# Attention and routed experts on one core: the first expert slot begins four query tiles later

## The chip, the cores and the metric

One core of one Trainium2 chip runs the whole kernel. The metric is the device time of one execution in microseconds (us); lower is better.

## The reference, cut to what is computed

```python
# attention: B=8 batches, H=8 heads, S=576 positions, D=64
scores = q @ k.T / sqrt(64)
scores = where(scores >= scores.max(-1) - 0.02, scores, -1e9)   # tau = 0.02
attn = softmax(scores); x = (attn @ v) -> [N=4608, DM=512]      # 8 heads side by side
# mixture of experts, one expert for each token: E=8, F=1024
logits = x @ w_gate + modality_bias[modality_id]                # [N, 8]
e = argmax(logits); g = softmax(logits)[e]
out[n] = g[n] * (relu(x[n] @ w1[e]) @ w2[e])
```

## The kernel before, in words

**Attention.** The work goes by head pairs, 32 of them (p = 0 to 31, four to a batch), and each pair by nine query tiles, so there are 288 tiles (or steps) n = 9p + i. For each tile TensorE computes the scores into one of two PSUM tiles (`qk_half`, L391), VectorE takes their maximum (`softmax_a`, L419, L421), ScalarE the exponential (L424), VectorE the product with the mask (`softmax_b`, L437). TensorE then transposes the result (`tr`, L465; ScalarE copies it, L475), and later multiplies it with v (`pv_half`, L499). Tiles 2 to 97 run two at a time: L391 and L465 of both, then one block of other matmuls, until the next two.

**Preparing a pair.** q and k of the next pair are loaded (`load_qk`, L116, L118), transposed on TensorE (L314 for the remainder, L329 for the main part), copied out by ScalarE (L316, L317, L332), and split on GpSimd into a high and a low half (`split_pool`, L302 and L303: tiles `nk`, `nq`, `qb`). Four DMAs on SyncE's queue put the halves of k (`km<-nk`, L338) and four those of q (`q<-nq`, L341) where the L391 matmuls of the next pair read them. Pair 7 begins with tile 63.

**From attention to experts.** Finished rows of x go to DRAM (`xs`, L558, L571). When a batch is done, its tokens are routed: the gate (L583 on), the counts, and five indirect DMAs of GpSimd that scatter each token's row number and weight into a table ordered by expert (`tab`, L651). `pick` chooses the expert with the most tokens left.

**Slots.** A slot gives one expert up to 256, 320 or 512 tokens of a batch while attention goes on: seven slots, the first two with 256 (batch 1) and 320 (batch 2) tokens, the rest with 512; what is left follows after attention. `slot()` builds a slot's work: `expert` (L763) reads the expert's number into a register; `rows` (L767, L769) loads the rows of the table (`tb<-tab`); `gather(t)` (L781) fetches 128 tokens of x with an indirect DMA of GpSimd (`xg<-xs,tb`); `xt(t)` (L795) transposes them; `wload` (L805 for w1, L809 for w2) loads a weight block into one of 4 `raw` buffers; `wsplit` (L825, L827) splits it on GpSimd into high and low halves, tiles `w1h`, `w1l` with 3 buffers each and `w2h`, `w2l` with 5; `l1` (L841) and `l2` (L868) are the matmuls. For the first slot these are 48 *pieces*: 32 of l1 (8 blocks f0 to f7, four pieces each, three matmuls of 256 columns a piece) and 16 of l2 (three matmuls of 512 columns). L852 and L853 turn a finished block of l1 into `hh` and `hl`.

**What sets the order.** Each engine runs its instructions in the order in which the program writes them, and nothing reorders them; so an instruction that waits holds back all that stands behind it on its engine, the DMAs that it issues included. What goes where in that order is set by a table `C` of numbers (L45 to L47): `at(t, f)` places work at step t, `put(n, f)` into the block after tile n. `begins` (L991) is the step at which each slot's pieces start: 64 for the first, 100 for the second. `draw` spreads a slot's pieces evenly over the steps from its begin to the next one's. Choosing, expert, rows, gathers and transposes stand at fixed distances ahead of the begin (L1026, L900 to L904), the weight blocks at those of the list `wS` or `wL` (L1052), each load `wl` = 3.5 steps ahead of its split.

Of the kernel before, what the change touches and what calls it, by code (L numbers as in the profile page):

```python
# [29 lines left out]
def tile_attn_moe(  # L30
# [13 lines left out]

    C = {'prep': [0, 1, 2], 'tr0': 6, 'pv0': 7, 'tr1': 12, 'sums': 13, 'pv1': 13, 'x': 14, 'gate': [15, 16, 17, 18], 'route': 18, 'routeb': 21, 'E0': 28, 'lag': 3, 'first': ((1, 0), (1, 1), (1, 2), (1, 3), (2, 0)), 'lld': {(1, 5): 15, (1, 6): 15.6, (1, 7): 16.2, (2, 5): 16.8, (2, 6): 17.4, (2, 7): 18}, 'late': ((1, 5), (1, 6), (1, 7), (2, 5), (2, 6), (2, 7)), 'pick': -14, 'vld': 6, 'qkld': -5, 'pre': 2.5, 'wl': 3.5, 'rows': -11, 'gat': [-9.5, -8.5, -7, -5], 'xt': [-6, -5, -4, -2], 'lc': 21, 't3': 84, 'neg': 1.0, 'draw': [2, 2, 2, 2, 1, 2, 2, 1, 2], 'last': 36, 'part': 84, 'join': 11, 'drawj': [2, 2, 2, 2, 2, 2, 0, 2, 2], 'gatej': [15, 15, 17, 18], 'te': 8, 'f0': 19, 'sc': 1, 'warm': 24,  # L45
         'wS': [-6, -4.7, -3.4, 3, 12.5, 14, 15.5, 21.5, 4.2, 5.4, 6.6, 7.5, 22.7, 23.8, 24.9, 25.8],
         'wL': [-5.5, -4, -2.5, 2.7, 12, 13.3, 14.6, 21, 3.8, 4.9, 6, 7.1, 15.8, 22.2, 23.4, 24.6], 'ask': 4, 'exp': -12.5, 'two': 98, 'end': (12, 13, (15, 16), (13.5, 13.6, 14.1, 14.2), 14.5, 15, 16.5), 'xf': 9, 'early': [], 'parts': ((((7, 0, 2), (9, 2, 5)), ((11, 0, 2), (13, 2, 5))), (((6, 0, 2), (8, 2, 4), (10, 4, 5)), ((12, 0, 2), (14, 2, 5)))), 'xp': ((15, 16), (16, 17)), 'prepp': ((0, 1, 2), (0, 0, 2)), 'trp': ((7, 11), (6, 12))}  # L47
    nc = tc.nc
    B, H, S, D = q.shape
    NE = wg.shape[1]  # L50
# [12 lines left out]
    W = 512  # L63
# [7 lines left out]
    SIDE = [(WH, 1), (WM, 2)] + [(W, b) for b in range(3, B)]  # L71
# [16 lines left out]
    xp = ctx.enter_context(tc.tile_pool(name="xp", bufs=1))  # L88
# [570 lines left out]
    def pick(w):  # L659

        a = tiny.tile([1, NE], F32, name="pk_a", bufs=1)
        nc.vector.scalar_tensor_tensor(out=a, in0=done, scalar=float(-U), in1=base[0][0:1, :],
                                       op0=ALU.mult, op1=ALU.add)
        nc.vector.scalar_tensor_tensor(out=a, in0=a, scalar=float(w), in1=iota_1, op0=ALU.is_ge, op1=ALU.mult)
        r = tiny.tile([1, 1], F32, name="pk_r", bufs=1)
        nc.vector.tensor_reduce(out=r, in_=a, axis=AX.X, op=ALU.max)
        nc.vector.tensor_scalar(out=a, in0=iota_1, scalar1=r, scalar2=None, op0=ALU.is_equal)
        t2 = tiny.tile([1, NE], F32, name="pk_d", bufs=1)
        nc.vector.scalar_tensor_tensor(out=t2, in0=a, scalar=float(U), in1=done, op0=ALU.mult, op1=ALU.mult)
        si = tiny.tile([1, 2], I32, name="pk_i")  # L670
        nc.vector.tensor_reduce(out=si[:, 1:2], in_=t2, axis=AX.X, op=ALU.max)
        nc.vector.tensor_scalar(out=si[:, 0:1], in0=r, scalar1=-1.0, scalar2=0.0, op0=ALU.add, op1=ALU.max)
        nc.vector.scalar_tensor_tensor(out=done, in0=a, scalar=float(w // U), in1=done, op0=ALU.mult, op1=ALU.add)
        return si[:, 0:1], si[:, 1:2]
# [73 lines left out]
    def slot(where, group, nrow, WT=W, wq=lambda: wp, nbuf=(4, 3, 5), lo_eng=None, xq=None, late=(), lined=False, pack=False):  # L748


        ev, pe, xts = [], [], []
        box = {}
        F2 = FC // 2
        TT = -(-WT // P)
# [21 lines left out]
        def gather(t):  # L776
            def f():
                xg = xt_pool().tile([P, DM], F32, name="xg", bufs=nx[1])
                box[("xg", t)] = xg

                nc.gpsimd.indirect_dma_start(  # L781
                    out=xg, out_offset=None, in_=xs[0:nrow, :],
                    in_offset=bass.IndirectOffsetOnAxis(ap=box["tb"][:, t, 0:1].bitcast(U32), axis=0),
                    bounds_check=nrow - 1, oob_is_err=False)
            return f

        def xt(t):
            def f():
                if t == 0:
                    room()  # L790
                ps = tbank()
                xg = box.pop(("xg", t))
                w = TP(t)
                for c in range(KC):
                    nc.tensor.transpose(out=ps[:, c * w:(c + 1) * w], in_=xg[0:w, c * P:(c + 1) * P],  # L795
                                        identity=ident[0:w, 0:w])
                ts = slice(t * P, t * P + w)
                split(ps[:, 0:KC * w].rearrange("a (c p) -> a c p", c=KC), box["xh"][:, :, ts], box["xl"][:, :, ts])
            return f
# [100 lines left out]
        else:  # L900
            ev += [(None, expert, C['exp']), (None, rows, C['rows'])]
        for t in range(TT):
            ev.append((t - 8, gather(t)) if xq else (None, gather(t), C['gat'][t - TT]))
            xts.append((C['xt'][t - TT] if not xq else t, xt(t)))  # L904
        for f_ in range(FC):
            t0 = (ta if f_ < F2 else tc_ - F2 * u1) + f_ * u1
# [16 lines left out]
        if xq:  # L923
            ev = [(e[0] - e[2], e[1]) if len(e) > 2 and e[0] > -8 else e for e in ev]
# [10 lines left out]
    PB = NPAIR * NI  # L935
# [5 lines left out]
    def at(t, f):  # L941
        events.setdefault(t, []).append(f)

    def put(n, *fs):
        extra.setdefault(n, []).extend(fs)

    for p in range(NPR):
        n0 = p * NI
# [39 lines left out]
            put(n0 + rb, lambda b=p // NPAIR: route_b(b))  # L988


    begins = [b * PB + C['E0'] + C['lag'] * max(0, z - 2) for z, (_, b) in enumerate(SIDE)]  # L991
    draw = [0] * (NSTEP + 2)
    for z, (w, _) in enumerate(SIDE):
        n0 = begins[z]
# [13 lines left out]
    def step_of(k):  # L1008

        if k >= upto[-1]:  # L1010
            return NSTEP + 2 + (k - upto[-1]) / 2
        n = bisect.bisect_right(upto, k) - 1
        return n + (k - upto[n]) / max(1, draw[n])
# [7 lines left out]
    for n0, (w, nb) in zip(begins, SIDE):  # L1021
        cells = {}

        def choose(cells=cells, w=w):
            cells["c"] = pick(w)
        at(n0 + C['pick'], choose)  # L1026
        late = C['late'] if n0 == begins[-1] else ()
        ev, pe, xts = slot(lambda cells=cells: cells["c"], lambda: group_bank(), nb * S, w, late=late)
        at(min(n0 - 0.45, NSTEP + 1), lambda pe=pe: work_q.extend(f for _, f in pe))
        for x, f in xts:  # L1030
            put(n0 + x, f)
        times = [t for t, _ in pe]
        k0 = sum(FC * KC + FC * -(-x // P) for x, _ in SIDE[:begins.index(n0)])

        def when(u):

            if u < 0:
                return n0 + u * C['neg'] * W / w
            k = bisect.bisect_right(times, u) - 1
            nxt = times[k + 1] if k + 1 < len(times) else times[k] + 0.5  # L1040
            x = k + min(1, (u - times[k]) / (nxt - times[k]))
            kf = math.floor(x)
            a, b = step_of(k0 + kf), step_of(k0 + kf + 1)
            return a + (x - kf) * (b - a) - 0.5
        for e in ev:

            if e[0] is None:
                t = n0 + e[2]
            elif n0 in begins[:-1]:

                which, f_ = e[3]
                t = n0 + C['w' + 'SL'[w == W]][8 * which + f_ - 8] - e[2]  # L1052
            elif e[2] and e[3] in C['lld']:
                t = NSTEP + C['lld'][e[3]]
            else:
                t = when(e[0]) - e[2] - (1.5 if e[3] in late and e[3][0] == 1 else 0)
            at(t, e[1])

    def last_slot(j, z):

        def where():
            si = fin["si"]
            return si[0:1, z, j:j + 1], si[0:1, z, MAXC + j:MAXC + j + 1]
        return slot(where, lambda: group_bank(), N, SIZES[z], lambda: fin["wp"], (8, 4, FC),
                    lambda which, f_: nc.vector if which == 1 else nc.gpsimd, (lambda: fin["xp"], (2, 4)),
                    lined=z + j == 0, pack=2 * SIZES[z] == W)
# [3 lines left out]
    def group_bank():  # L1070
        if "pm" in fin:
            return fin["pm"].tile([P, 512], F32, name="pm", tag="pm")
        return tbank(True)
# [18 lines left out]
    for z in range(3):  # L1092
        for j in range(ALWAYS[z]):
            for e in sum(last_slot(j, z), []):
                t = t0 + e[0] if len(e) == 2 else min(t0 + e[0], F0 + e[2])
                if z + j == 0 and getattr(e[1], "key", 0) in C['first']:
                    t = F0 - 8.15 + C['first'].index(e[1].key) / 1000
# [12 lines left out]
    with tc.manual_schedule(engines={ET.PE, ET.Pool}):  # L1110
# [5 lines left out]
        for n in range(NSTEP + LAG):  # L1116
# [8 lines left out]
            two = 2 <= n < C['two']  # L1125
# [82 lines left out]
```

## Time and profile before

| | us |
|---|---|
| median of 3 runs | 1025.12 (1023.4 to 1026.83) |
| the profiled execution: its own time | 1026.37 |
| the profiled execution: first to last instruction (span) | 1024.6 |
| PE (TensorE) busy in the span | 990.1 |
| VectorE, ScalarE, GpSimd busy | 687.6, 628.4, 534.2 |

The profile is of one execution. PE stands for the matmuls, PEld for TensorE's weight loads, DVE for VectorE, ACT for ScalarE, POOL for GpSimd, SPq for SyncE's issuing of DMAs; L391 is line 391 of the kernel. A row's time is counted from the span's start.

### The profile page before, as it was taken

The numbers are of one execution on the slowest core, as the hardware profiler recorded it, in microseconds if no ns is written. First come the engines' busy times: TensorE is split into PE (matmuls) and PEld (weight loads), VectorE is DVE, ScalarE is ACT, GpSimd is POOL, SyncE is SP. The second block draws the span as 40 slices with busy tenths as digits, with TensorE's granted clock in tenths as the row PEclk, the third lists the DMA queues.
The fourth block names the chain that finished last, engine by engine and source line by source line (L and its number), as shares of the span: only waits on it lengthen the run. The fifth ranks groups of instructions, "written<-read, shape, count | busy, mean of one in ns | idle before, by whom it ended". The sixth has DMA issues, their size and how long they took to land.

```text
span 1024.6 us, 20353 instructions
## 1 busy us (share of the span) xinstructions
PE 990.1 (97%) x6556; PEld 795.6 (78%) x6556; DVE 687.6 (67%) x1697; ACT 628.4 (61%) x1407; POOL 534.2 (52%) x781
## 2 busy tenths in 40 slices
PE   7999989999999999999999999999999999999996
PEld 6777768778877887888778887788778868888885
DVE  6888968787767776777687777777676765333422
ACT  6777767666666666666667666666666635334430
POOL 3363466386637554645555554646566363624311
PEclk9999999999999999999999999999999999999998
DMA  6677586668657766586646566767666236634301
GB/s 153 141 164 168 121 188 170 173 151 205 174 131 161 202 158 151 105 218 155 171 115 158 138 165 148 143 155 205 159 118 173 79 111 171 221 104 146 108 15 43
DMA packets 207315, 152.10 MB, mean 148 GB/s; under 512 B 100510, under 2 KB 168094, under 8 KB 207200
## 3 DMA queue, kind: packets, MB, share of 16 engines
q1 hardware_dynamic: 200000, 131.53, 53.1%
q0 software_dynamic: 7200, 19.18, 6.0%
q8 instruction: 54, 0.88, 0.4%
q14 instruction: 61, 0.50, 0.2%
HBM read 80.06 MB, written 19.48 MB: 97 GB/s over the span
## 4 chain that ended last, share of the span: by engine, by line
PE 78%; DVE 9%; issue 8%; ACT 3%; POOL 1%; DMA 0%; another core or an unknown queue 0%; POOLq 0%; ACTq 0%; DVEq 0%
PE bk L499 16%; PE s L391 15%; PE bk L841 11%; PE bk L465 10%; PE bk L868 9%; PE pm L868 5%; PE pm L841 5%; DVE nm L419 3%; DVE pr L437 3%; PE bk L329 2%; ACT e L424 2%; PE bk L490 1%; PE bk L795 1%; PE bk L551 1%; PE bk L583 1%
## 5 line engine op out<-in xcount | busy, mean ns | idle before, releaser
L419 DVE TENSOR_REDUCE nm<-s 128x1 f32<-128x576 f32 x288 | 216.3, 753 | 113.3 <-PE s L391 106.7
L437 DVE SCALAR_TENSOR_TENSOR pr<-s,nm,e 128x576 f32<-128x576 f32 x288 | 231.7, 815 | 65.2 <-ACT e L424 56.8
L424 ACT ACTIVATE e<-s,nm 128x576 f32<-128x576 f32 x288 | 214.3, 744 | 67.1 <-DVE nm L419 55.8
L391 PE MATMUL s<-km,q 128*128 128x288 f32 x1024 | 197.0, 314 | 11.1 <-DVE pr L437 7.2
L475 ACT COPY ptm<-bk 128x512 f32<-128x512 f32 x256 | 149.3, 583 | 54.9 <-PE bk L465 50.2
L465 PE MATMUL bk<-ident,pr 128*128 128x128 f32 x1152 | 174.0, 273 | 0.5 <-DVE hl L853 0.3
L391 PEld LDWEIGHTS s<-km,q 128*128 128x128 f32 x1024 | 147.1, 189 | 27.8 <-DVE pr L437 16.6
L465 PEld LDWEIGHTS bk<-ident,pr 128*128 128x128 f32 x1152 | 140.0, 140 | 30.0 <-issue 7.2
L499 PE MATMUL bk<-ptm,v_m 128*64 128x320 f32 (+1 forms) x1024 | 141.1, 412 | 2.5 <-DVE hl L853 2.5
L827 POOL TENSOR_TENSOR w2l<-raw,w2h 128x512 fp32r<-128x512 f32 x77 | 98.3, 1285 | 31.8 <-ACT w2h L823 27.7
L499 PEld LDWEIGHTS bk<-ptm,v_m 128*64 128x64 f32 x1024 | 68.5, 137 | 53.1 <-issue 8.1
L883 POOL DMA_INDIRECT out_dram<-y,tb x37 | 38.0, 1026 | 123.4 <-DVE y L881 89.7
L454 ACT COPY rp<-pr 128x64 f32<-128x64 f32 x271 | 59.9, 248 | 43.6 <-DVE pr L437 37.2
L302 POOL CAST nk<-str 128x64 fp32r<-128x64 f32 x31 | 7.4, 238 | 146.6 <-ACT str L316 144.9
L841 PE MATMUL bk<-xh,w1h 128*128 128x512 f32 (+2 forms) x204 | 82.4, 404 | 0.0
L841 PE MATMUL bk<-xl,w1h 128*128 128x512 f32 (+2 forms) x204 | 74.1, 363 | 0.0
L841 PE MATMUL bk<-xh,w1l 128*128 128x512 f32 (+2 forms) x204 | 74.0, 363 | 0.0
L868 PE MATMUL bk<-w2h,hh 128*128 128x512 f32 x168 | 73.7, 439 | 0.0
L827 POOL TENSOR_TENSOR w1l<-raw,w1h 128x512 fp32r<-128x512 f32 x53 | 68.0, 1283 | 4.2
L868 PE MATMUL bk<-w2l,hh 128*128 128x512 f32 x168 | 66.4, 395 | 0.0
L868 PE MATMUL bk<-w2h,hl 128*128 128x512 f32 x168 | 66.3, 394 | 0.0
L421 DVE TENSOR_SCALAR nm<-nm,ntau 128x1 f32<-128x1 f32 (+1 forms) x271 | 58.1, 224 | 4.3
(201 smaller groups left out, 1887.5 us busy)
## 6 DMA issues: line engine op xcount, KB each, us to landing
raw<-in_moe_w_dram SPq DMA_DIRECT2D x160, 256.0 KB
q<-nq SPq DMA_DIRECT2D x124, 256.0 KB
km<-nk SPq DMA_DIRECT2D x124, 144.0 KB
v_m<-in_v_dram SPq DMA_DIRECT2D x32, 256.0 KB
xs<-xr SPq DMA_DIRECT2D x32, 256.0 KB
k_m<-in_k_dram SPq DMA_DIRECT2D x62, 128.0 KB
q_m<-in_q_dram SPq DMA_DIRECT2D x62, 128.0 KB
vr<-in_v_dram SPq DMA_DIRECT2D x64, 16.0 KB
```

The lines of the kernel that those rows point to most:

```text
L391: nc.tensor.matmul(out=sps[:, hf, 0:SH], lhsT=a, rhs=x, start=(z == 0), stop=(z == len(passes) - 1))
L419: in_line(nc.vector.tensor_reduce(out=nm[:, 0:1], in_=sv, axis=AX.XY, op=ALU.max, negate=True), two)
L421: in_line(nc.vector.tensor_scalar(out=nm2[:, 1, cols(y)], in0=nm2[:, 0, cols(y)], scalar1=-1.0, scalar2=ntau, op0=ALU.mult, op1=ALU.add), two)
L424: in_line(nc.scalar.activation(out=e, in_=sv, func=AF.Exp, bias=nm[:, 0:1]), two and n < LEAD)
L437: in_line(nc.vector.scalar_tensor_tensor(out=pr.rearrange("p (a x) -> p a x", a=2), in0=s2[n % 2][:, :, 0:SH], scalar=nm[:, 1:2], in1=e, o ...
L454: (nc.gpsimd.tensor_copy if 2 <= n < 46 else nc.scalar.copy)(out=state[("rp", p)][:, 2 * c + s + x, :], in_=pr[:, SA:S])
L465: nc.tensor.transpose(out=ps[:, kc * P:(kc + 1) * P], in_=pr[:, kc * P:(kc + 1) * P], identity=ident)
L475: in_line(nc.scalar.copy(out=ptm[:, s, :, (c % 2) * P:(c % 2 + 1) * P], in_=pv), n + 2 < LEAD)
L499: nc.tensor.matmul(out=o, lhsT=lhsT, rhs=rhs, start=start, stop=stop, skip_group_check=True)
L827: then(eng.tensor_tensor(out=lo, in0=raw, in1=hi.bitcast(F32), op=ALU.subtract), eng is nc.vector and (lined or late))
L841: nc.tensor.matmul(out=ps[:, 0:WT], lhsT=a[:, cs], rhs=x[:, c, :], start=(c == 0 and z == 0), stop=(c == KC - 1 and z == 2))
L868: nc.tensor.matmul(out=ps, lhsT=h[:, ts], rhs=w, start=(z == 0 and y == 0), stop=(z == F2 - 1 and y == 2))
```

## The change: what it does

The first slot begins at step 68 in place of 64, with the same 48 pieces up to step 99. The expert is still chosen at step 50 (`pick0`); reading its number and the table's rows move from steps 51.5 and 53 to 55.5 and 57, the two gathers from 57 and 59 to 59 and 59.1, the transposes from the blocks of 60 and 62 to those of 64 and 66. The weight blocks get a list of their own, `wS0`: f0 to f2 of w1 are split at steps 59.5, 60.5, 61.5 (58, 59.3, 60.6 before), f3 at 71.7 (67 before), f4 to f7 and w2's blocks, but for a tenth of a step, where they were. The loads follow, 3.5 steps ahead. All other slots keep their numbers.

```diff
--- before.py
+++ after.py
@@ -44,7 +44,7 @@
 
     C = {'prep': [0, 1, 2], 'tr0': 6, 'pv0': 7, 'tr1': 12, 'sums': 13, 'pv1': 13, 'x': 14, 'gate': [15, 16, 17, 18], 'route': 18, 'routeb': 21, 'E0': 28, 'lag': 3, 'first': ((1, 0), (1, 1), (1, 2), (1, 3), (2, 0)), 'lld': {(1, 5): 15, (1, 6): 15.6, (1, 7): 16.2, (2, 5): 16.8, (2, 6): 17.4, (2, 7): 18}, 'late': ((1, 5), (1, 6), (1, 7), (2, 5), (2, 6), (2, 7)), 'pick': -14, 'vld': 6, 'qkld': -5, 'pre': 2.5, 'wl': 3.5, 'rows': -11, 'gat': [-9.5, -8.5, -7, -5], 'xt': [-6, -5, -4, -2], 'lc': 21, 't3': 84, 'neg': 1.0, 'draw': [2, 2, 2, 2, 1, 2, 2, 1, 2], 'last': 36, 'part': 84, 'join': 11, 'drawj': [2, 2, 2, 2, 2, 2, 0, 2, 2], 'gatej': [15, 15, 17, 18], 'te': 8, 'f0': 19, 'sc': 1, 'warm': 24,
          'wS': [-6, -4.7, -3.4, 3, 12.5, 14, 15.5, 21.5, 4.2, 5.4, 6.6, 7.5, 22.7, 23.8, 24.9, 25.8],
-         'wL': [-5.5, -4, -2.5, 2.7, 12, 13.3, 14.6, 21, 3.8, 4.9, 6, 7.1, 15.8, 22.2, 23.4, 24.6], 'ask': 4, 'exp': -12.5, 'two': 98, 'end': (12, 13, (15, 16), (13.5, 13.6, 14.1, 14.2), 14.5, 15, 16.5), 'xf': 9, 'early': [], 'parts': ((((7, 0, 2), (9, 2, 5)), ((11, 0, 2), (13, 2, 5))), (((6, 0, 2), (8, 2, 4), (10, 4, 5)), ((12, 0, 2), (14, 2, 5)))), 'xp': ((15, 16), (16, 17)), 'prepp': ((0, 1, 2), (0, 0, 2)), 'trp': ((7, 11), (6, 12))}
+         'wL': [-5.5, -4, -2.5, 2.7, 12, 13.3, 14.6, 21, 3.8, 4.9, 6, 7.1, 15.8, 22.2, 23.4, 24.6], 'ask': 4, 'late0': 4, 'pick0': -18, 'wS0': [-8.5, -7.5, -6.5, 3.7, 8.5, 10, 11.5, 17.5, 0.2, 1.4, 2.6, 3.4, 18.7, 19.8, 20.9, 21.8], 'gat0': [-9, -8.9], 'exp': -12.5, 'two': 98, 'end': (12, 13, (15, 16), (13.5, 13.6, 14.1, 14.2), 14.5, 15, 16.5), 'xf': 9, 'early': [], 'parts': ((((7, 0, 2), (9, 2, 5)), ((11, 0, 2), (13, 2, 5))), (((6, 0, 2), (8, 2, 4), (10, 4, 5)), ((12, 0, 2), (14, 2, 5)))), 'xp': ((15, 16), (16, 17)), 'prepp': ((0, 1, 2), (0, 0, 2)), 'trp': ((7, 11), (6, 12))}
     nc = tc.nc
     B, H, S, D = q.shape
     NE = wg.shape[1]
@@ -900,7 +900,7 @@
         else:
             ev += [(None, expert, C['exp']), (None, rows, C['rows'])]
         for t in range(TT):
-            ev.append((t - 8, gather(t)) if xq else (None, gather(t), C['gat'][t - TT]))
+            ev.append((t - 8, gather(t)) if xq else (None, gather(t), C['gat0' if TT == 2 else 'gat'][t - TT]))
             xts.append((C['xt'][t - TT] if not xq else t, xt(t)))
         for f_ in range(FC):
             t0 = (ta if f_ < F2 else tc_ - F2 * u1) + f_ * u1
@@ -988,7 +988,7 @@
             put(n0 + rb, lambda b=p // NPAIR: route_b(b))
 
 
-    begins = [b * PB + C['E0'] + C['lag'] * max(0, z - 2) for z, (_, b) in enumerate(SIDE)]
+    begins = [b * PB + C['E0'] + C['lag'] * max(0, z - 2) + (0 if z else C['late0']) for z, (_, b) in enumerate(SIDE)]
     draw = [0] * (NSTEP + 2)
     for z, (w, _) in enumerate(SIDE):
         n0 = begins[z]
@@ -1023,7 +1023,7 @@
 
         def choose(cells=cells, w=w):
             cells["c"] = pick(w)
-        at(n0 + C['pick'], choose)
+        at(n0 + C['pick0' if n0 == begins[0] else 'pick'], choose)
         late = C['late'] if n0 == begins[-1] else ()
         ev, pe, xts = slot(lambda cells=cells: cells["c"], lambda: group_bank(), nb * S, w, late=late)
         at(min(n0 - 0.45, NSTEP + 1), lambda pe=pe: work_q.extend(f for _, f in pe))
@@ -1049,7 +1049,7 @@
             elif n0 in begins[:-1]:
 
                 which, f_ = e[3]
-                t = n0 + C['w' + 'SL'[w == W]][8 * which + f_ - 8] - e[2]
+                t = n0 + C['wS0' if n0 == begins[0] else 'w' + 'SL'[w == W]][8 * which + f_ - 8] - e[2]
             elif e[2] and e[3] in C['lld']:
                 t = NSTEP + C['lld'][e[3]]
             else:
```

How this moves work on the engines: first on GpSimd, at the steps around 57 to 60. `nk_167` and `nq` are the halves of k and q of pair 7; L781 are the first slot's gathers.

```order
 L303 TENSOR_TENSOR nk_167<-st,nk_167 128x512
-L781 DMA xg<-xs,tb 128x512
-L302 CAST nq<-st 128x512
-L303 TENSOR_TENSOR nq<-st,nq 128x512
-L825 CAST w1h<-raw 128x512
-L827 TENSOR_TENSOR w1l<-raw,w1h 128x512
-L781 DMA xg<-xs,tb 128x512
+L302 CAST nq<-st 128x512
+L303 TENSOR_TENSOR nq<-st,nq 128x512
+L781 DMA xg<-xs,tb 128x512 x2
+L825 CAST w1h<-raw 128x512
+L827 TENSOR_TENSOR w1l<-raw,w1h 128x512
```

One gather stood ahead of q's split and one behind it; now both stand behind it, and the first weight block behind them.

On SyncE, at the same steps (`tb<-tab` is the load of the table's rows, L571 stores x, L805 loads a w1 block):

```order
+L805 ISA
+L805 DMA raw<-in_moe_w_dram 128x4x128
+L571 DMA xs<-xr 64x128
 L767 TENSOR_LOAD pk_i
 L767 ISA x2
 L769 ISA
 L769 DMA tb<-tab 128x2x2
-L571 DMA xs<-xr 64x128
-L805 ISA
-L805 DMA raw<-in_moe_w_dram 128x4x128
```

One weight load and the store now leave ahead of the table's load. Behind it stood three weight loads ahead of the DMAs L116, L118, L338 and L341 of pair 7; now one does, and the third stands behind those of q.

On TensorE and GpSimd, some 25 steps on: the block w1 f4 of the first slot is the tile `w1h_2646` before and `w1h_2630` after. Here is TensorE before, from the end of the block after tile 85 (its last lines L499 on `oh1_130` are the routing's counts):

```order
L499 MATMUL bk2_180<-oh1_130,ones_bf_113 128x8
L841 MATMUL bk3_181<-xh_2096,w1h_2646 128x256
L841 MATMUL bk3_181<-xl_2097,w1h_2646 128x256
L841 MATMUL bk3_181<-xh_2096,w1l_2647 128x256
L499 MATMUL bk0_178<-ptm1_2695,v_m_2362 64x320 x8
L499 MATMUL bk0_178<-ptr1_2893,vr0_87 64x320 x2
L841 MATMUL bk1_179<-xh_2096,w1h_2687 128x256
```

and after, from the two tiles 86 and 87 that follow that block:

```order
L391 MATMUL s0_172<-km1_165,q21_163 128x288 x4
L465 MATMUL bk0_178<-ident_105,pr_2952 128x128 x4
L391 MATMUL s1_173<-km1_165,q21_163 128x288 x4
L465 MATMUL bk3_181<-ident_105,pr_2954 128x128 x4
L841 MATMUL bk1_179<-xh_2211,w1h_2630 128x256
L841 MATMUL bk1_179<-xl_2212,w1h_2630 128x256
L841 MATMUL bk1_179<-xh_2211,w1l_2631 128x256
L841 MATMUL bk1_179<-xh_2211,w1h_2630 128x256
L841 MATMUL bk1_179<-xl_2212,w1h_2630 128x256
L841 MATMUL bk1_179<-xh_2211,w1l_2631 128x256
L551 MATMUL bk2_180<-ident_105,ot_2743 128x128 x4
```

The last read of f4 was in the block after tile 85 and is now in the block after 87. GpSimd after, where the split of f7 (`w1h_2998`, the third tile of w1 after f4's, so the next owner of its buffer) stands, as it did before, between q's split and the scatters:

```order
L303 TENSOR_TENSOR nq_2895<-st_2893,nq_2895 128x512
L825 CAST w1h_2998<-raw_2833 128x512
L827 TENSOR_TENSOR w1l_2999<-raw_2833,w1h_2998 128x512
L651 DMA tab_157<-pay_147,posi_2971 37888x2 x5
L825 CAST w2h_3045<-raw_2848 128x512
L827 TENSOR_TENSOR w2l_3046<-raw_2848,w2h_3045 128x512
```

Its place on GpSimd is the same in both kernels; what moved is the last read of the buffer that it takes over.

## Rows read from the trace of the kernel before

**Rows 1.** The page: busy time and share of each engine, with instructions.

```profile
PE 990.1 (97%) x6556; PEld 795.6 (78%) x6556; DVE 687.6 (67%) x1697; ACT 628.4 (61%) x1407; POOL 534.2 (52%) x781
```

**Rows 2.** Timeline, PE, 118 to 160: start, busy, what, count [idle before <- what ended it].

```profile
138.78 1.08 PE L795 MATMUL bk<-ident,xg 128*128 128x128 f32 x4 [2.47 <-ACT rp L454]
...
145.71 0.77 PE L391 MATMUL s<-km,q 128*128 128x288 f32 x4 [1.74 <-issue]
...
146.86 0.60 PE L795 MATMUL bk<-ident,xg 128*128 128x128 f32 x4
...
150.03 0.77 PE L391 MATMUL s<-km,q 128*128 128x288 f32 x4
...
154.91 0.28 PE L841 MATMUL bk<-xh,w1h 128*128 128x256 f32 x1
...
155.27 0.69 PE L391 MATMUL s<-km,q 128*128 128x288 f32 x4
```

**Rows 3.** Timeline, SPq (DMA issues), 118 to 150.

```profile
130.18 0.40 SPq L769 DMA_DIRECT2D tb<-tab  x1
...
131.38 2.37 SPq L805 DMA_DIRECT2D raw<-in_moe_w_dram  x3
...
134.60 2.71 SPq L338 DMA_DIRECT2D km<-nk  x4
...
138.12 3.28 SPq L341 DMA_DIRECT2D q<-nq  x4
```

**Rows 4.** Waits of SPq, 118 to 150: total us, times, longest.

```profile
SPq L769 <- DMA tab<-pay,posi: 7.0, 1, 7.0
```

**Rows 5.** Timeline, POOL, 124 to 162.

```profile
131.69 1.28 POOL L303 TENSOR_TENSOR nk<-st,nk 128x512 fp32r<-128x512 f32 x1
133.12 1.08 POOL L781 DMA_INDIRECT xg<-xs,tb  x1 [0.15 <-issue]
...
134.91 1.27 POOL L303 TENSOR_TENSOR nq<-st,nq 128x512 fp32r<-128x512 f32 x1
...
138.24 1.04 POOL L781 DMA_INDIRECT xg<-xs,tb  x1
```

**Rows 6.** Windows: busy PE, PEld, DVE, ACT, POOL; granted clock, DMA share, GB/s.

```profile
134.00:138.00 4.00, 2.31 (x18) 1.97 (x16) 3.40 (x9) 3.29 (x9) 3.83 (x5) 1.00 0.95 268
138.00:142.00 4.00, 3.22 (x16) 2.58 (x18) 1.70 (x4) 1.23 (x4) 3.68 (x6) 0.57 1.00 208
...
217.50:219.00 1.50, 1.43 (x14) 1.00 (x16) 1.50 (x5) 0.90 (x3) 1.42 (x3) 1.00 0.51 76
```

**Rows 7.** DMA view, 136 to 146: packets, MB, share of the engines, by queue.

```profile
q1 hardware_dynamic: 1793, 1.84, 86.6%
q0 software_dynamic: 137, 0.43, 16.6%
```

**Rows 8.** Timeline, POOL, 198 to 240.

```profile
206.85 0.61 POOL L825 CAST w1h<-raw 128x512 fp32r<-128x512 f32 x1
...
208.98 1.06 POOL L651 DMA_INDIRECT tab<-pay,posi  x1 [0.16 <-DVE pk_a L662]
...
224.65 0.24 POOL L302 CAST nk<-str 128x64 fp32r<-128x64 f32 x1 [1.75 <-ACT str L316]
...
228.77 1.06 POOL L781 DMA_INDIRECT xg<-xs,tb  x1 [0.15 <-DMA kq_r<-in_k_dram]
```

**Rows 9.** Timelines, PE, 200 to 207 and 207 to 240.

```profile
204.85 0.36 PE L841 MATMUL bk<-xh,w1h 128*128 128x256 f32 x1
...
210.52 0.37 PE L841 MATMUL bk<-xh,w1h 128*128 128x256 f32 x1
...
217.57 1.95 PE L499 MATMUL bk<-ptm,v_m 128*64 128x256 f32 x16 [2.49 <-DVE hl L853]
...
233.36 0.50 PE L868 MATMUL bk<-w2h,hh 128*128 128x512 f32 x1
...
234.29 0.63 PE L795 MATMUL bk<-ident,xg 128*128 128x128 f32 x4
```

## The prediction, made before the changed kernel was run

> **What bounds the kernel now.** I read the page first, then the timelines of PE, SPq and POOL around the first slot's start (118 to 160) and around the second slot's (198 to 240), the waits of SPq, and the busy time by stretch. PE is busy for 990.1 of 1024.6 us [rows 1], so PE's own order sets the time, and a change can only gain where PE stands still or runs at the lower clock, or lose by new holes in it. The first slot's start has two holes [rows 2]: 2.47 us ahead of L795 at 138.78, the first transposes of the gathered tokens, and 1.74 us ahead of L391 at 145.71, the first score matmul of pair 7 (tile 63), which the profile puts down to "issue". I put the second down to q's DMAs: they are issued at 138.12 to 141.40 [rows 3], and L391 reads what they bring.
>
> Why q leaves so late is to be read on SPq. It stood 7.0 us at the load of the table's rows, L769, until the scatters had landed [rows 4]; that load left at 130.18, and behind it came three weight loads (131.38), km at 134.60 and q at 138.12 [rows 3]. k's split on POOL was ready at 131.69 + 1.28 = 132.97; the gather at 133.12 then stood between it and q's split, which ended at 134.91 + 1.27 = 136.18 [rows 5]. In 138 to 142 the DMA engines were full (share 1.00, 208 GB/s) and the granted clock was 0.57, near the lower level of 1.2 GHz, after PE's idle time; in 134 to 138 it was 1.00 [rows 6].
>
> **The change, part by part.** PE's total work stays the same: 48 pieces are 48 pieces. What can change is where PE waits.
>
> *The first transposes leave the block of tile 62.* PE then no longer waits 2.47 us for the gather there, nor does the 1.08 us of L795. Taken alone this is worth nothing: the next thing on PE is tile 63, and it waits for q. Before, PE was through with its work at 145.71 - 1.74 = 143.97. Without the hole, L795 and the half clock (4 us at 0.57 lose 1.7, of which I count 1.1 beyond L795's part), it would be through near 139.3, and wait there.
>
> *q's DMAs.* km no longer has two of the three weight loads ahead of it on SPq. It can leave when k's split is done, near 133.05 in place of 134.60, and q near 136.3 in place of 138.12: 1.8 us earlier (q's split, with no gather ahead of it, ends near 135.1 and doesn't decide). Against this, the second gather moves from 138.24 to about 136.3, into the time of km and q. Its 128 rows of 512 floats are 256 KB, and at 208 GB/s [rows 6] that is 1.26 us of all engines, which leaves 0.6. One weight load, also 256 KB, moves behind q; if q had waited for it in full the gain would be 1.9. It was issued one to three us ahead of km, so it was mostly out of the way. I take 1.2, between 0.6 and 1.9: tile 63 starts near 144.5.
>
> That the gathers share the engines with q is what the DMA view shows [rows 7]: in 136 to 146 queue q1 (SyncE's) took 86.6% of the engines and q0 (GpSimd's) 16.6%, both at once. The Trainium skill says so too (DMA: Bandwidth & Descriptors, Queues, rings and completion order): each engine takes turns between the queues that it has work for, packet by packet. By that rule standing behind q's split on POOL gives q no precedence over the gathers; the trace agrees, and a reading of the change by which q is served first would give 1.8 or 1.9 here in place of 1.2.
>
> *Tiles 64 to 67.* Five pieces leave these tiles; one piece takes 155.27 - 154.91 = 0.36 [rows 2], so 1.8 us leave. Two groups of L795 come in, 0.60 each as the second one before: 1.2. Net 0.6 less. The second group also leaves the block before tile 64 (0.60), but the softmax chain covers part of that: I take half, 0.3.
>
> *The clock.* PE would now stand still for about 5 us (139.3 to 144.5) in one piece. After 2.47 us of it the clock was 0.57 for 4 us [rows 6], which costs 1.7; after another hole of 2.49 us, ahead of L499 at 217.57 [rows 9], it was 1.00 [rows 6]. Bounds 0 to 1.7; I take 0.4, since PE has waits of its own at that pair's start. So by tile 68: -1.2 - 0.9 + 0.4 = **-1.7 us**, from -3.2 to +0.5 with the bounds above.
>
> *Repaying.* At tile 68 five pieces are owed. They are spread over tiles 68 to 99; by tile 87 about two have been made up: +0.7, so the changed kernel stands at **-1.0** there.
>
> *The split of f7 and what is behind it.* This is the term that decides. w1's high halves have three buffers, and f7 takes f4's. Before, f4's last piece on PE was at 204.85 [rows 9], and f7's split on POOL at 206.85 waited for nothing [rows 8]. After, the block of tile 85 still reads f4, and so does the one behind tiles 86 and 87: in before's times two pieces from 210.52 on [rows 9], so the last read ends near 211.2. POOL's order there is the same, so POOL stands from 206.85 to 211.2: **4.35 us**, a wait that is not in the trace of before. Queued behind it on POOL: five scatters of batch 2's table (208.98 on), four splits of w2 blocks, the small splits of pair 11, and the gathers of the second slot (228.77) [rows 8]. POOL's only slack on the way is 1.75 us ahead of 224.65, where it waited for ScalarE. The first gather is then late by 4.35 - 1.75 = **2.6 us**. On SyncE the second slot's table load, which waits for the scatters, is late by up to 4.35, and km and q of pair 11 by 2.6 with POOL's split.
>
> Is there slack between that gather and PE? It was issued at 228.77, and L795 on PE began at 234.29 [rows 9], 5.5 us later, with no wait of PE shown. The first slot's gather took 138.78 - 133.12 = 5.66 with PE waiting for it [rows 2, 5]. So I take the slack as nothing (at most 2.6, if a gather lands in 3): the 2.6 us become a hole in PE. In addition one piece of l2, 0.9 us (233.36 to 234.29 [rows 9]), stood ahead of L795 and now stands behind it, so it can't fill the hole: +0.9. The rest that is owed is made up within POOL's delay or that hole. Sum: -1.0 + 2.6 + 0.9 = **+2.5 us**. From there the two kernels do the same work in the same order, and PE, which is the bound, has no place to give it back.
>
> The profiled execution took 1026.37, 1.25 above the median of the runs; 1026.37 + 2.5 = 1028.9 by it, and **1027.6** by the median. What a measurement of this kernel can tell from no change is about 0.3%, 3.1 us.
>
> **Rivals.**
> - *No hole at the second slot.* The gather lands in about 3 us, so its 5.5 us held 2.6 of slack. Then only -1.0 + 0 stays: 1024.1, at most 1025 with the piece that is moved. For it: PE shows no wait ahead of 234.29. Against: the 5.66 us of the first slot's, with full engines.
> - *q lands early, and no hole.* SPq issued the last of q's DMAs until 141.40, and L391 ran 4.3 us later. If the lighter load brings it down 2 us after its issue at 139.6, tile 63 begins near 141.6: -4.1 there, -0.9 in tiles 64 to 67, +0.7 repaid, no clock loss; with the slack of the case above -4.3, with the moved piece -3.4: 1020.8 to 1021.7. Against it: the full engines in 138 to 142.
> - *Slower: the clock.* PE stands still longer than before in one piece at both places (5 us ahead of tile 63, 3.5 at the second slot's L795). If the granted clock falls to the lower level for 4 us after each, that is 1.7 twice in place of the 0.4: 2.5 - 0.4 + 3.4 = +5.5, 1030.6. It decides from the point where the stretch after both holes shows a clock near 0.5. For it: 0.57 after 2.47 us of idle time; against: 1.00 after 2.49 us. The Trainium skill (TensorE: Matmul & The Clock Gate, HAM oscillation) says that a wait for a DMA between groups of matmuls throttles TensorE again, and the next group starts slow; by that rule this rival's +5.5 would be the sum, and the trace agrees at one of the two holes only.
>
> **How the numbers follow.** Forecast (+2.5, give or take 2: 1025.6 to 1029.6) 0.42; no hole 0.19; early q without a hole 0.17; the clock 0.22. Within 3.1 us of 1025.12 lies up to 1028.2: 0.26 of the forecast, nearly all of "no hole" (0.17), 0.02 each of the last two cases: 0.47. Slower: 0.16 + 0.20 = 0.36. Faster: 0.02 + 0.15 = 0.17. The range is 1021.5 to 1031.0: it holds the forecast, no hole, half of the early q, and most of the clock's case.
>
> **What would show it.** In the changed kernel's trace: L391 of pair 7 waits 4 to 6 us and begins 0.6 to 1.9 us earlier relative to the tiles before it; the two gathers of the first slot run back to back behind nq's L303; L825 of w1 ahead of the five scatters L651 shows an idle time of about 4.4 us put down to PE; the second slot's first L781 stands 2 to 3 us later relative to PE's tiles, and L795 behind it has an idle time of 2 to 3.5 us. I am wrong if that L825 doesn't wait, if L795 of the second slot doesn't, or if pair 7 starts more than 3 us earlier than it did.

## The result, and the profile after

| | before | changed |
|---|---|---|
| median, us (9 runs each) | 1025.12 (1023.4 to 1026.83) | 1032.5 (1028.72 to 1033.69) |
| ratio, 95% interval | 1 | 1.006 (1.0045 to 1.0074) |
| profiled execution: its time, span | 1026.37, 1024.6 | 1033.69, 1031.7 |

By the ratio the change makes the kernel slower by 0.6%, 6.2 us; the two medians stand 7.4 us apart. The measured median lies above the range that was given. The profiled execution is the slowest of its nine, 1.2 us above the median. PE's work on the page stays about what it was [rows 1]; its time without work grew from 34.5 to 39.3 us:

```profile
PE 992.4 (96%) x6556; PEld 797.7 (77%) x6556; DVE 687.3 (67%) x1697; ACT 629.6 (61%) x1407; POOL 533.7 (52%) x781
```

At tile 58 the two profiles agree to 0.03 us (its L391 began at 130.20 before, at 130.17 after), so times on from there can be laid side by side. First PE's timeline (118 to 165) at tiles 58, 63, 64 and 68, to be held against [rows 2], and SPq's (118 to 155), against [rows 3]:

```profile
130.17 0.79 PE L391 MATMUL s<-km,q 128*128 128x288 f32 x4
...
145.10 1.30 PE L391 MATMUL s<-km,q 128*128 128x288 f32 x4 [5.73 <-issue]
...
151.06 0.78 PE L391 MATMUL s<-km,q 128*128 128x288 f32 x4
...
160.25 0.80 PE L391 MATMUL s<-km,q 128*128 128x288 f32 x4
```

Before, tiles 58 and 68 (110 to 150 and 150 to 190):

```profile
130.20 0.80 PE L391 MATMUL s<-km,q 128*128 128x288 f32 x4
...
159.88 0.69 PE L391 MATMUL s<-km,q 128*128 128x288 f32 x4
```

SPq in the changed kernel:

```profile
131.11 0.40 SPq L769 DMA_DIRECT2D tb<-tab  x1
...
134.27 2.51 SPq L338 DMA_DIRECT2D km<-nk  x4
...
137.53 4.05 SPq L341 DMA_DIRECT2D q<-nq  x4
```

Tile 63 starts 0.6 us earlier than before, with one wait of 5.73 in front; q left only 0.6 earlier, because the table's load left 0.9 later. Tile 64 is 1.0 later than before and tile 68, at 160.25, 0.4 later: the wait was followed by the lower clock. The stretches (columns as in [rows 6]) behind tile 63 and, 90 us on, behind the second slot's first transposes:

```profile
145.00:148.00 3.00, 2.90 (x13) 2.40 (x15) 1.56 (x4) 0.71 (x2) 0.00 (x0) 0.50 1.26 204
148.00:151.00 3.00, 3.00 (x16) 1.68 (x13) 1.71 (x8) 1.44 (x7) 1.27 (x2) 0.50 0.81 224
...
238.00:240.00 2.00, 1.82 (x7) 1.66 (x8) 0.08 (x1) 0.59 (x1) 1.84 (x3) 0.50 1.18 239
240.00:242.00 2.00, 2.00 (x7) 1.61 (x6) 0.61 (x1) 0.00 (x0) 1.92 (x3) 0.50 1.05 221
```

And POOL (200 to 262) and PE (200 to 248) where f7 is split and where the second slot begins, against [rows 8, 9]:

```profile
212.41 0.61 POOL L825 CAST w1h<-raw 128x512 fp32r<-128x512 f32 x1 [5.46 <-PE bk L841]
...
214.55 1.06 POOL L651 DMA_INDIRECT tab<-pay,posi  x1 [0.16 <-DVE hl L853]
...
228.44 0.24 POOL L302 CAST nk<-str 128x64 fp32r<-128x64 f32 x1
...
232.53 1.06 POOL L781 DMA_INDIRECT xg<-xs,tb  x1 [0.15 <-DMA k_m<-in_k_dram]
```

```profile
209.54 0.79 PE L391 MATMUL s<-km,q 128*128 128x288 f32 x4
...
238.18 1.09 PE L795 MATMUL bk<-ident,xg 128*128 128x128 f32 x4 [5.00 <-DMA xg<-xs,tb]
...
241.62 1.16 PE L391 MATMUL s<-km,q 128*128 128x288 f32 x4
```

Before, tiles 86 and 96:

```profile
208.68 0.69 PE L391 MATMUL s<-km,q 128*128 128x288 f32 x4
...
235.47 0.70 PE L391 MATMUL s<-km,q 128*128 128x288 f32 x4
```

This is the chain that the prediction described. f7's split waits 5.46 us for PE's last read of f4; the scatters begin at 214.55 in place of 208.98; the slack of 1.75 us ahead of nk's small split is gone; the second slot's first gather leaves at 232.53 in place of 228.77; and PE stands 5.00 us ahead of L795. Tile 96 (the L391 behind it) begins at 241.62 in place of 235.47, 6.15 us late, where tile 68 was 0.4 late. From there nothing is given back: from tile 96 to the end all 14 profiles of this case take 788.1 to 790.1 us, while tile 96 begins anywhere from 230.29 to 241.62.

### The profile page after: what moved, and what is told of

Read it like the earlier page. It is cut to its first block, busy times and chain, and to the rows that moved or that the text cites. A ratio compares the mean times of both kernels' runs of the same rounds, so it can differ in the third digit from the quotient of the medians.

```text
span 1031.7 us, 20360 instructions
## 1 busy us (share of the span) xinstructions
PE 992.4 (96%) x6556; PEld 797.7 (77%) x6556; DVE 687.3 (67%) x1697; ACT 629.6 (61%) x1407; POOL 533.7 (52%) x781
## 4 chain that ended last, share of the span: by engine, by line
PE 72%; DVE 10%; issue 8%; DMA 4%; ACT 2%; POOL 2%; SPq 1%; POOLq 0%; DVEq 0%; ACTq 0%
PE bk L499 14%; PE s L391 14%; PE bk L841 10%; PE bk L465 10%; PE bk L868 9%; PE pm L868 4%; PE pm L841 3%; DVE pr L437 3%; DVE nm L419 3%; PE bk L329 2%; PE bk L795 1%; PE bk L490 1%; ACT e L424 1%; PE bk L551 1%; DMA xg<-xs,tb 1%
## 5 line engine op out<-in xcount | busy, mean ns | idle before, releaser
L437 DVE SCALAR_TENSOR_TENSOR pr<-s,nm,e 128x576 f32<-128x576 f32 x288 | 231.5, 815 | 66.0 <-ACT e L424 61.5
L391 PE MATMUL s<-km,q 128*128 128x288 f32 x1024 | 198.2, 315 | 14.8 <-DVE pr L437 8.5
L475 ACT COPY ptm<-bk 128x512 f32<-128x512 f32 x256 | 149.4, 584 | 56.2 <-PE bk L465 55.5
L391 PEld LDWEIGHTS s<-km,q 128*128 128x128 f32 x1024 | 147.9, 190 | 32.6 <-DVE pr L437 20.6
L465 PEld LDWEIGHTS bk<-ident,pr 128*128 128x128 f32 x1152 | 140.8, 140 | 29.7 <-issue 7.1
L499 PE MATMUL bk<-ptm,v_m 128*64 128x320 f32 (+1 forms) x1024 | 141.6, 414 | 0.0
L499 PEld LDWEIGHTS bk<-ptm,v_m 128*64 128x64 f32 x1024 | 68.6, 137 | 50.4 <-issue 8.1
```

Of the source, the lines that this page charges most:

```text
L391: nc.tensor.matmul(out=sps[:, hf, 0:SH], lhsT=a, rhs=x, start=(z == 0), stop=(z == len(passes) - 1))
L437: in_line(nc.vector.scalar_tensor_tensor(out=pr.rearrange("p (a x) -> p a x", a=2), in0=s2[n % 2][:, :, 0:SH], scalar=nm[:, 1:2], in1=e, o ...
L465: nc.tensor.transpose(out=ps[:, kc * P:(kc + 1) * P], in_=pr[:, kc * P:(kc + 1) * P], identity=ident)
L475: in_line(nc.scalar.copy(out=ptm[:, s, :, (c % 2) * P:(c % 2 + 1) * P], in_=pv), n + 2 < LEAD)
L499: nc.tensor.matmul(out=o, lhsT=lhsT, rhs=rhs, start=start, stop=stop, skip_group_check=True)
```

## The experiments

The theory under test, **W**: f7's split waits for f4's buffer and holds back the scatters and the second slot's gathers. Rivals: **S** or **G**, the loss lies in the first slot's start, with both gathers behind q's split; and that the half clock costs nothing. Each ratio is to the kernel before on the same chip. The runs stood on three chips, on which before had medians of 1027.48, 1024.30 and 1024.38.

**f7's split alone put behind the scatters** (its load keeps its place among the DMAs, its use too):

```diff
-'wS0': [-8.5, -7.5, -6.5, 3.7, 8.5, 10, 11.5, 17.5, ...
+'wS0': [-8.5, -7.5, -6.5, 3.7, 8.5, 10, 11.5, 18.6, ...
```

> The change, with the split of w1's block f7 in the first slot put behind the five scatters on GpSimd. Theory W (f7's split waits 5.5 us for f4's buffer and holds back the scatters and the second slot's gathers): the second slot's first L781 is 3 to 4 us earlier, L795 behind it waits under 1 us in place of 5.0, the granted clock stays at 1.00 after it, and the time falls from 1032.5 to about 1025.5 (1024 to 1027.5). Rival S (the loss is in the first slot's start, its gathers behind q's split and the half clock at tile 63): the time stays at 1031 or above.

Measured: ratio 0.9988 (0.997 to 1.0005), median 1025.82. Its timelines of POOL (200 to 250) and PE (218 to 248):

```profile
206.70 1.06 POOL L651 DMA_INDIRECT tab<-pay,posi  x1 [2.09 <-DVE pk_a L664]
...
212.90 0.62 POOL L825 CAST w1h<-raw 128x512 fp32r<-128x512 f32 x1
...
227.20 1.06 POOL L781 DMA_INDIRECT xg<-xs,tb  x1 [0.16 <-DMA raw<-in_moe_w_dram]
```

```profile
233.49 0.60 PE L795 MATMUL bk<-ident,xg 128*128 128x128 f32 x4
...
235.33 0.69 PE L391 MATMUL s<-km,q 128*128 128x288 f32 x4
```

The scatters no longer wait for PE, f7's split finds its buffer free, and L795 has no wait at all. This speaks for W and against S; the changed kernel had not run on that chip.

**The kernel before with GpSimd held back at the same place:**

```diff
-                    nc.gpsimd.tensor_copy(out=hi, in_=raw)
+                    [nc.gpsimd.tensor_copy(out=hi, in_=raw) for _ in range(9 if (WT, which, f_) == (256, 1, 7) else 1)]
```

> The kernel before, with the cast of w1's block f7 in the first slot done nine times in place of once, which holds GpSimd back by 8 x 0.69 = 5.5 us at the place where the changed kernel waits 5.46. Nothing else is moved. Theory W: the second slot's first L781 is 3.8 us later, L795 waits 3.5 to 4.5 us, the granted clock falls to about 0.5 for some 4 us behind it, and the time is 1030 to 1032. Rival S: a wait on GpSimd there is hidden, and the time stays within 1 us of 1025.1.

Measured: 1030.84, ratio 1.0033 (1.0019 to 1.0047): slower, by 3.4 us, while W's count was 5 to 7. Timelines of PE (218 to 248) and POOL (200 to 250), and the stretch 226 to 230:

```profile
222.99 0.33 PE L314 MATMUL bk<-ident,kq_r 128*128 128x128 f32 x1 [1.91 <-ACT ot L522]
...
238.73 0.63 PE L795 MATMUL bk<-ident,xg 128*128 128x128 f32 x4 [0.70 <-DMA xg<-xs,tb]
```

```profile
207.61 6.07 POOL L825 CAST w1h<-raw 128x512 fp32r<-128x512 f32 x9
...
233.16 1.06 POOL L781 DMA_INDIRECT xg<-xs,tb  x1
```

```profile
226.00:230.00 4.00, 3.70 (x16) 3.67 (x17) 2.60 (x7) 1.78 (x4) 3.76 (x7) 0.50 0.74 195
```

Holding GpSimd back there does slow the kernel, and the first gather is late as W said (233.16). But the wait at L795 was 0.70, not 3.5 to 4.5: in this run PE had lost its time earlier, in a stall ahead of L314 and at the lower clock in 226 to 230. Before has no profile on that chip, so whether it stalls there too is not shown. So it confirms the chain up to the gather, and says that PE's lateness and the gather's don't add: the later of the two counts.

**Only the gathers put back** (one ahead of q's split):

```diff
-'gat0': [-9, -8.9]
+'gat0': [-10.9, -9]
```

> The change, with the first slot's gathers where they were before: one ahead of q's split on GpSimd, one behind it. Theory W: this place decides under 1.5 us; tile 63 starts 0 to 1 us later than in the changed kernel (145.1), and the time stays between 1031.5 and 1033.5. Rival S: the time goes back to 1028 or below.

Measured: ratio 1.0003 (0.9985 to 1.0022), which is outside of W's 1031.5 to 1033.5 and near S; tile 63, too, began earlier than the 145.1 of the changed kernel and not later, at 142.25. But its trace showed f7's wait of 5.42 as in the changed kernel, and the changed kernel hadn't run on that chip. So the question stayed open until both ran side by side, below.

**TensorE kept busy through both waits**, with 95 small matmuls at the first of them (cut shown) and 85 ahead of L795 (not shown; here the transposes stand at L801):

```diff
+        if n == 63 and hf == 0:
+            for _ in range(95):
+                nc.tensor.matmul(out=sps[:, 0, 0:P], lhsT=zero, rhs=zero, start=True, stop=True, skip_group_check=True)
```

> The change, with 95 small matmuls on zeros added ahead of tile 63's scores and 85 ahead of the second slot's first transposes, so that TensorE works through both waits (5.7 and 5.0 us). They write PSUM that the next matmul overwrites. If the half clock behind the two waits costs what the trace shows (0.50 for 6 us behind tile 63, about 4.5 us behind L795), the clock stays at 1.00 there and the time falls by 3.5 to 5 us, to 1027.5 to 1029. If the clock costs nothing, because other engines set the pace there, the time stays within 1 us of 1032.5.

Measured: 1029.08, ratio 1.0029 (1.0007 to 1.005). f7's wait was again 5.46. The stretches behind tile 63 and behind L795 (at 237.14 here):

```profile
145.00:148.00 3.00, 3.00 (x36) 2.47 (x33) 1.58 (x4) 0.72 (x2) 0.00 (x0) 1.00 1.04 230
...
238.00:242.00 4.00, 3.82 (x28) 3.38 (x28) 2.77 (x5) 2.26 (x5) 2.68 (x3) 1.00 1.06 201
```

The clock stays at 1.00 at both places. But the added matmuls lasted longer than the waits (PE 222 to 244, POOL 195 to 240):

```profile
232.38 4.92 PE L799 MATMUL bk<-zero 128*128 128x128 bf16 x85
237.14 0.60 PE L801 MATMUL bk<-ident,xg 128*128 128x128 f32 x4
```

```profile
229.40 1.06 POOL L784 DMA_INDIRECT xg<-xs,tb  x1
```

Where PE waited for this gather, the profiles show 4.8 to 5.9 us from its issue to the transposes; here it is 7.7, so by an estimate from these numbers PE was held some 2 us beyond the gather. At tile 63 it is the same: from the issue of q's first DMA it took 9.57 us, and 7.3 to 7.6 in five profiles with the gathers in the same place and a wait ahead of tile 63. So this run does not price the clock. On its chip the kernel with f7's wait and the lower clock (gathers put back) measured 1.0003, and no gain from the kept clock can be told.

**The changed kernel once more**, and three variants of the one with f7's split moved, on one chip.

> The changed kernel once more, beside the next three and the kernel before on one chip. In its first profile tile 64 began 16.0 us after tile 62, in the two runs of the same code up to there with other parts changed it was 14 us. Theory V (that start varies from run to run, by when the scatters land): the ratio to before is 1.001 to 1.004, and tile 64 begins about 14 us after tile 62. Theory F (it is a property of the changed kernel): ratio 1.0045 to 1.0075 as first measured, tile 64 at 15.5 or more. In both the split of f7 waits 5.4 to 5.5 us on GpSimd, and L795 of the second slot waits 2 us or more.

Measured: ratio 1.0066 (1.0046 to 1.0085), theory F's number; in the profiled run, the fastest of its four, tile 64 began 14.05 us after tile 60, theory V's number. (The tile that the expectation calls 62 is tile 60; counted from it, the first profile has 17.0 and not 16.0.) So the start does vary, and yet the loss is a property of the kernel: L795 waited 4.71 us there too.

> The change with f7's split behind the scatters and the first slot's gathers where they were before (one ahead of q's split). If each repair works by itself and the gathers' place decides nothing, the ratio to before is as with f7's split moved alone, 0.9988, within 0.0015; if the first gather ahead of q's split is worth something more, 0.997 or below.

Measured: 1.0003 (0.9987 to 1.0019). No gain from the gathers' place can be told on top of the moved split.

The third puts the two gathers behind the splits of f0 and f1 (`'gat0': [-6.9, -6.8]`):

> The change with f7's split behind the scatters and the first slot's two gathers behind the splits of f0 and f1 on GpSimd, some 4 us later than in the changed kernel. Theory Q (gathers and q share the DMA engines, so that each 256 KB moved out of q's way is worth up to 1.2 us): tile 63's wait falls by 1 to 2.5 us, the half clock behind it gets shorter or goes, and the ratio is 0.996 to 0.998. If q's landing hangs on its own issue alone: tile 63 as in the run with f7's split moved alone, and the ratio 0.9988 within 0.0015.

Measured: 1022.15, ratio 0.9978 (0.9963 to 0.9992). Timelines of PE and POOL, 134 to 155:

```profile
133.91 0.80 PE L391 MATMUL s<-km,q 128*128 128x288 f32 x4
...
141.36 1.18 PE L391 MATMUL s<-km,q 128*128 128x288 f32 x4 [2.14 <-issue]
```

```profile
138.45 1.08 POOL L781 DMA_INDIRECT xg<-xs,tb  x1 [0.15 <-DMA k_m<-in_k_dram]
```

Tile 63 begins 141.36 - 133.91 = 7.5 us after tile 60; with f7's split moved alone it was 9.2 (144.08 - 134.93), and in both runs the table's load left 0.3 us before tile 58's scores. The gathers had shared the engines with q. This speaks for theory Q, by one profile of each.

> The change with f7's split behind the scatters and 65 small matmuls on zeros ahead of tile 63's scores (they write PSUM that the next matmul overwrites), which take about 3.7 us of the wait there. If the half clock behind that wait sets the pace of tiles 63 to 65: granted clock 1.00 in the 6 us behind it, and the ratio falls by 0.001 to 0.002 below 0.9988. If VectorE, ScalarE or q's successor set it: the clock is 1.00 and the ratio stays within 0.001 of 0.9988.

Measured: 0.9999 (0.9989 to 1.001). Against 0.9988 on another chip and 1.0003 for the second variant on the same one, no gain can be told: what the clock at tile 63 alone is worth is less than these intervals resolve.

**The four that decide, on one chip:**

> The changed kernel beside the next three and the kernel before on one chip, since the runs so far stood on different chips. Both theories: ratio 1.004 to 1.007.

> The change with only the first slot's gathers put back (one ahead of q's split), which gave a ratio of 1.0003 on another chip. Theory W (the wait of f7's split decides, the gathers' place under 1.5 us): ratio within 0.0015 of the changed kernel's on this chip. Theory G (both gathers behind q's split cost some 4 us): ratio 0.003 or more below it.

> The change with only f7's split put behind the scatters, on the same chip. Theory W: 0.005 to 0.0075 below the changed kernel's ratio, at 0.998 to 1.0. Theory G: less than 0.003 below it.

| | median, us | ratio, 95% interval |
|---|---|---|
| before | 1024.38 | 1 |
| changed | 1029.44 | 1.0061 (1.0041 to 1.0081) |
| changed, gathers put back | 1029.63 | 1.0054 (1.0033 to 1.0074) |
| changed, f7's split behind the scatters | 1024.91 | 1.0008 (0.9997 to 1.0019) |

The gathers' place makes no difference that can be told; the 1.0003 of the run on the other chip was not repeated. There PE had lost time ahead of L795, in the stall of the last section (5.85 us from tile 91 to tile 92, here 3.37), and then waited 2.18 us at L795, here 4.75; that this is all of the difference is not shown. f7's split is worth 0.0053 by the ratios, 5.4 us; by the medians it is 4.5. In the profile with the gathers put back the chain is as in the changed kernel (POOL and PE, 200 to 250 and 218 to 248):

```profile
211.12 0.61 POOL L825 CAST w1h<-raw 128x512 fp32r<-128x512 f32 x1 [5.46 <-PE bk L841]
```

```profile
236.66 1.09 PE L795 MATMUL bk<-ident,xg 128*128 128x128 f32 x4 [4.75 <-DMA xg<-xs,tb]
```

PE from tile 86 to tile 96, in the changed kernel (200 to 246) and with f7's split moved:

```profile
204.75 0.79 PE L391 MATMUL s<-km,q 128*128 128x288 f32 x4
...
232.95 1.09 PE L795 MATMUL bk<-ident,xg 128*128 128x128 f32 x4 [4.57 <-DMA xg<-xs,tb]
...
236.40 1.16 PE L391 MATMUL s<-km,q 128*128 128x288 f32 x4
```

```profile
207.52 0.79 PE L391 MATMUL s<-km,q 128*128 128x288 f32 x4
...
231.39 0.63 PE L795 MATMUL bk<-ident,xg 128*128 128x128 f32 x4
...
233.26 0.69 PE L391 MATMUL s<-km,q 128*128 128x288 f32 x4
```

The stretch takes 31.65 us with f7's wait and 25.74 without, 5.9 less, whatever the start of the slot did before it.

Last, the late gathers with 40 small matmuls ahead of tile 63:

> A candidate to beat both kernels: the change with f7's split behind the scatters, the first slot's two gathers behind the splits of f0 and f1, and 40 small matmuls on zeros ahead of tile 63's scores (2.3 us; they write PSUM that the next matmul overwrites). Without these matmuls the ratio was 0.9978. If the half clock behind tile 63 costs what 4 us near 0.7 lose, about 1 us more is gained: 0.9965 to 0.9975, granted clock 1.00 in the 6 us behind tile 63. If not: 0.9978 within 0.0008.

Measured: 1022.3, ratio 0.9974 (0.9959 to 0.9988). The clock behind tile 63 was 1.00:

```profile
141.00:144.00 3.00, 2.75 (x25) 1.84 (x22) 2.20 (x6) 1.34 (x4) 0.00 (x0) 1.00 1.06 246
```

It beats both kernels, by 0.26% to before and 0.9% to the changed one; that the matmuls add to the 0.9978 without them is not shown.

## Why the prediction was wrong

The mechanism that the prediction named as the deciding one is the cause: with f7's split moved alone, the loss is gone. What failed was the term for the clock behind the hole, put at 0, and the sizes of others, nearly all in one direction.

- **The wait of f7's split**: 4.35 us predicted, 5.46 measured. GpSimd came to it at the same time as before (206.95), but PE's last read of f4 was some 1.2 later than the 211.2 that the working reckoned; 0.9 of this is that tile 86 began at 209.54 and not at 208.68.
- **The first gather**: 2.6 us late predicted; 232.53 - 228.77 = 3.8 measured, 2.9 against the start of tile 86. About right: the slack on the way was a little more than the 1.75 that was read. Taking the slack between this gather and PE as nothing was right too: wherever PE waited for it, 4.8 to 5.9 us lay between its issue and L795.
- **The hole in PE**: 2.6 + 0.9 = 3.5 predicted, 5.00 measured. PE came to it earlier than reckoned: before, PE had stood 2.49 us ahead of 217.57 [rows 9], and the step counted that as spent time. It was no part of the change. In the changed run that stall did not come, PE reached L795 earlier, and waited longer. That stall had hidden how near the gather was to being late: in the five profiles with f7's split moved and no such stall, L795 waits 0 to 1.45 us.
- **The clock behind that hole, the step that failed outright**: priced at 0 in the sum and given to a rival. Measured 0.50 in 238 to 242. From L795 to tile 96 it took 3.44 us, and 1.84 for the same work at 1.00 (235.33 - 233.49, f7's split moved): 1.6 for the clock. Before showed one hole of 2.47 followed by 0.57 and one of 2.49 followed by 1.00 [rows 6], and the working gave no reason for 0 behind a hole that it had itself computed as longer, 3.5. The rival with its +5.5 (1030.6) comes nearest to the 1032.5, but it was put beside the hole as an alternative with 0.22. In all five profiles with f7's wait and no added matmuls a hole of 2.18 to 5.00 stands ahead of L795, and the clock falls to 0.50 behind each; behind those of up to 1.45 in the other kernels it stays at 1.00.
- **The start**: -1.7 by tile 68 predicted; +0.4 in the first profile. In four more profiles of kernels that are the same up to there, from the start of tile 58's scores to that of tile 68's, it took 26.3 to 29.7 us, before 29.68: -3.4 to 0.0. The predicted value lies among these, but two of the four are of the fastest runs of the changed kernel on their chips. That it varies by 3 us from run to run was not foreseen, and the first profile was of the worst start. (Two small slips: the first L795 left the block behind tiles 60 and 61, not that of tile 62, and the bound of -3.2 adds up to -3.1.)
- **q's landing**: 1.2 earlier predicted, 0.6 in the first profile. That the gathers share the engines with q, and that standing behind q's split gives q no precedence, was right: 4 us more between them brought tile 63 forward by 1.7 (9.2 to 7.5). The Trainium skill (DMA: Bandwidth & Descriptors, Queues, rings and completion order) says the same of the shared engines, and this pair of profiles agrees.
- **"No hole" and "early q"** did not come; with f7 moved, the kernel is where "no hole" put it (1024.1 predicted; 1024.9 and 1025.8 measured).

On HAM oscillation (the Trainium skill, TensorE: Matmul & The Clock Gate) the measurements now agree at both places of the changed run: 0.50 behind a wait of 5.73 us and behind one of 5.00.

Together, by the first profile: L795 came 238.18 - 234.29 = 3.9 late, where -1.0 + 2.6 = 1.6 was predicted. Of the 2.3 between, 1.9 is the start (tile 86 at +0.9 in place of -1.0), 0.3 the gather (2.9 late against the start of tile 86 in place of 2.6) and 0.1 its landing (5.65 us from issue to L795 in place of 5.52). From L795 to tile 96 it took 3.44 us in place of 1.18: 1.84 - 1.18 = 0.7 is the piece of l2 that now stands there (0.9 predicted), and 1.6 the half clock. 3.9 + 0.7 + 1.6 is the 6.15 (to rounding) by which tile 96 was late.

How much of f7's wait is hole and how much clock can be read from the two profiles of tiles 86 to 96 on one chip: the wait at L795 is 4.57 us against none, and from L795 to tile 96 it is 3.45 against 1.87, 1.6 for the clock; 0.3 is made up elsewhere. That a kept clock would give these 1.6 back is not shown by a run.

Open: the first profile's start took 3 to 4 us more than those of the changed kernel on two other chips, and yet the ratios there are the same. Those two profiles are of the fastest runs, and before has no profile on those chips; its one trace has a stall of 2.49 us in it that the changed kernel's don't have.

## What to carry to other kernels

When pieces of work are spread later, look up which buffers they free later, and who takes these over: a split that stands ahead of unrelated work on an in-order engine makes everything behind it wait for the latest reader. A hole that a change opens on TensorE can have its price in the clock behind it as well; then the two are added, not set against each other. And what a profile shows as no wait may be the work of a stall elsewhere in that one run: the slack is known only when both sides' times are explained.

## What the runs showed of the hardware that was not expected

- **The scatters' landing varies.** In runs of the same code up to there, SPq's table load, which waits for the five scatters, left 7.5 to 9.3 us after the last of them was issued. Against the start of tile 58 it left at +0.94 us in the first profile (131.11) and at -0.83 in the fastest run of the changed kernel, and tile 63 began 14.93 and 12.57 us after tile 58: q's queue passes the lateness on. That run's SPq and PE:

```profile
128.34 0.40 SPq L769 DMA_DIRECT2D tb<-tab  x1
```

```profile
129.17 0.80 PE L391 MATMUL s<-km,q 128*128 128x288 f32 x4
...
141.74 1.09 PE L391 MATMUL s<-km,q 128*128 128x288 f32 x4 [3.37 <-issue]
```

- **A stall of some 2 to 3 us of PE behind the scatters.** Before (2.49 on PE, 2.64 on ScalarE with "remote" as its releaser) and four other profiled runs have it (ScalarE idle for 2.36 to 4.74), all four on one chip; the first changed run and all profiles on the other two chips don't, also where the same kernel had it. Nothing here explains it.
